# Two transformer layers on one core: fixed instruction orders, 76 instead of 50 score tiles on VectorE, elementwise work shared with GpSimd

## The chip, the cores and the metric

The kernel runs on one core of one Trainium2 chip. The metric is device microseconds from launch to end. TensorE (PE in the profile), ScalarE (ACT), VectorE (DVE), GpSimd (POOL) and SyncE (SP) each take their own list of instructions in order; semaphores connect the lists.

## The reference

`x` has 2048 rows of 448, in bf16. Attention has 16 heads of 28.

```python
x = A_x
x = x + _A_ref(_layernorm(x), A_wqkv, A_wo)              # attention
x = x + _B_ref(_layernorm(x), B_w1, B_w2, B_w3, B_w4)    # token mixer, MLP
...
scores = jnp.einsum("bhqd,bhkd->bhqk", q, k) * (Dh ** -0.5)
p = _softmax(scores, axis=-1)
o = jnp.einsum("bhqk,bhkd->bhqd", p, v)
...
h = _gelu(_layernorm(x) @ w1)       # then four column groups, shifted by -1, 1, -2, 2 rows
x1 = x + hs                         # hs = shifted h @ w2
h2 = _gelu(_layernorm(x1) @ w3) @ w4
return x1 + h2
```

The pair of lines on `x` is done twice, with the same weights: layers 0 and 1.

## The kernel before, in words

**Work.** The 2048 rows are 16 tiles of 128. Layer by layer, rows are normed, transposed and projected to qT, kT (heads in strips of 32 partitions, four heads to a group g) and vaug (v with a column of ones, which gives the softmax sum). Queries are taken in units u of 512 rows (the last 512 of the last layer in halves of 256). A segment is one unit, one group of four heads and a range of keys. For each 128 keys and each head PE makes a score tile of 128 keys by 512 queries (L1243); the tile is exponentiated into PT in bf16; PE multiplies it with vaug and gathers the result in bank 5 (L1318). When a segment ends, `t_norm` takes the sums out, transposes them, divides, and `t_outproj` multiplies by `wo` and adds to `x_res`. Then the mixer (`t_mixA`: norm, w1, gelu by `tanh_gelu`; `t_x1`: w2, norm) and the MLP (`t_mixB`: w3, gelu in place on ScalarE, w4) follow for that unit, while the attention of the next unit or the next layer runs.

**Exponentials.** Score tiles go in groups of alternately three and two into PSUM banks 0 to 2 and 3 to 4 (bank 5 takes the sums); one ScalarE instruction exponentiates a group (L1269), 128x1536 or 128x1024. In some groups of three the third tile is taken by VectorE instead (`t_dexp`, L1156): L1159 reads the bank and makes an integer of the score, L1166 cuts out its fraction, L1167 and L1168 evaluate a cubic, L1172 puts the bf16 bits together in PTD. ScalarE then has a 1024-column instruction for that group. `OFFL` and `on_dve` (L1132) choose these groups: every sixth or eighth in some ranges, 50 in all. Scores of group n+2 go into the banks of group n, the third only after L1159 has read its tile.

**Order.** All steps are generators that yield operations with the engine, an assumed duration, and what they read and write. `Sched.run` (L319) takes the operations greedily, in an order of due times that two rounds of planning give (`latest_starts`); `MOVES` and `perturb` (L455) shift due times by recorded random numbers. Buffers and PSUM banks are taken in the order in which the planner gets to them. `Plan.finalize` then sets the semaphores; there is no wait but for a true dependency, so SP and the others run ahead as far as their list and its waits allow. `keep_pe_busy` (L291) fills planned gaps of PE with products of ones (L1686, 128x256), at most to 0.8 of a window of 4 us.

**POOL before** makes the -1/2 powers of the norms (L1028, L1447, L1470, L1568), some masks and memsets. Norms of rows are L886 (`norm_x`), L1473, L1542 and L1572, residual adds L1392, L1570 and L1633, the division L1365, and the tanh polynomial L1419, L1420 and L1422 with L1437 after ScalarE's tanh (L1433), all on VectorE. `mm` (L665, L668) records the plain products, as one of 128 columns or, when PE is in column mode, as four of 32.

**Loads.** SP issues in order: x of the first four tiles, wk, wq, wv, the rest of x; later `wo` and the weights of mixer and MLP at given segments (`t_setup2`).

Of the kernel before, what the change touches and what calls it, by code (L numbers as in the profile page):

```python
# [17 lines left out]
class _Op:  # L18
    __slots__ = ("eng", "fn", "deps", "sig", "cnt", "waits", "dma", "ekey", "vc", "sem", "t_end", "pos", "every", "oid", "dur", "lft", "lst")

    def __init__(self, eng, fn, dma):
# [16 lines left out]
        self.lst = None  # L38


def _split(acc):
    if isinstance(acc, tuple) and len(acc) == 2 and isinstance(acc[0], tuple):
        return acc
    return acc, None


class Plan:
# [67 lines left out]
    def finalize(self, nc, stack):  # L115
# [4 lines left out]
        nd = 0  # L120
        for e in ENGS:
# [28 lines left out]
    def emit(self, eng_name, e):  # L150
        for op in self.ops[eng_name]:
# [5 lines left out]
            if isinstance(inst, list):  # L157
                first, inst = inst[0], inst[-1]
# [9 lines left out]
class Sched:  # L168
# [8 lines left out]
    def __init__(self, P):  # L177
# [4 lines left out]
        self.pe_mode = None  # L182
        self.act_tab = None
# [8 lines left out]
        self.fill = None  # L192
        self.recent = []
        self.clock = 0.0
        self.plan = None
        self.moves = []
# [3 lines left out]
    def spawn(self, gen, prio=5, order=None, parent=None):  # L200
        self.seq += 1
        if parent is None:
            tid = (self.seq,)
        else:
            parent[7] += 1
            tid = parent[6] + (parent[7],)
        self.tasks.append([prio, self.seq if order is None else order + self.seq * 1e-6, gen, None, None, False, tid, 0, 0, None])

    def rank(self, t):
        if self.plan is None:  # L210
            return (t[0], t[1])
        return (self.plan.get((t[6], t[8]), 1e9), t[1])
# [4 lines left out]
    def _advance(self, t, force=False):  # L217
        changed = False
        while True:
# [39 lines left out]
            elif c == "acq":  # L259
# [22 lines left out]
                t[4] = got  # L282
# [8 lines left out]
    def keep_pe_busy(self, until):  # L291
        if self.fill is None:
            return
        dur, fn, banks, key, reads = self.fill
        while self.cur["pe"] + dur + 0.12 < until:
# [21 lines left out]
            self.pe_mode = "plain"  # L317

    def run(self):  # L319
        P = self.P  # L320
        while True:
            while self.moves and self.clock >= self.moves[0][0]:
                self.perturb(self.moves.pop(0)[1])
# [23 lines left out]
            for t in self.tasks:  # L347
# [5 lines left out]
                for a in kw0.get("alt", ()):  # L353
                    cands.append(a)
# [8 lines left out]
                for ci, (eng, dur, fn, kw) in enumerate(cands):  # L363
# [13 lines left out]
                    if ci > 0 and (self.cur[eng] > ready + 0.05 or eng in self.reserved):  # L377
                        continue
# [57 lines left out]
            op = P.add(eng, fn, reads, writes, kw.get("deps", ()), dma, t_end)  # L436
            self.live.update(k for k in (_split(a)[0] for a in writes) if k[0] == "ps")
            self.live.difference_update(kw.get("last", ()))
            op.oid = (t[6], t[8])
# [15 lines left out]
    def perturb(self, seed):  # L455
        rng = random.Random(seed)
        if rng.random() < 0.2:
            self.SLACK = rng.choice((0.0, 0.06, 0.12, 0.3))
            self.TOL = rng.choice((0.0, 0.5, 1.5, 4.0))
            self.EPS = rng.choice((0.02, 0.05, 0.12))  # L460
        t = self.clock - self.shift
        lo, hi = t - 30.0, t + rng.choice((10.0, 25.0, 50.0, 90.0))
        depth = rng.choice((0, 1, 2, 3, 9, 9))
        width = rng.choice((1.0, 3.0, 8.0, 20.0))
        frac = rng.choice((0.05, 0.2, 0.5, 1.0))
        plan = self.plan
        sh = {}
        for k, v in plan.items():
            if lo < v < hi and k is not None:
                g = k[0][:depth] if depth else k  # L470
                d = sh.get(g)
                if d is None:
                    d = sh[g] = rng.gauss(0, width) if rng.random() < frac else 0.0
                if d:
                    plan[k] = v + d
# [21 lines left out]
def build_kernel(nc, A_x, A_wqkv, A_wo, B_x, B_w1, B_w2, B_w3, B_w4, out, n_layers=2):  # L497
    S = A_x.shape[1]
    D = 448
# [12 lines left out]
    OFFL = ((48, 104, 6), (104, 300, 6), (372, 411, 6), (480, 520, 6), (520, 600, 8), (640, 731, 6))  # L512
# [6 lines left out]
    MOVES = [  # L519
        [  # L520
# [50 lines left out]
    def c_f2b(n):  # L571
        return 0.07 + n * 0.00052
# [1204 lines left out]
```

## Time and profile before

| | us |
|---|---|
| median of three runs | 1059.28 |
| lowest and highest | 1057.09, 1060.65 |
| profiled execution, first to last instruction | 1059.8 |
| PE busy | 1020.3 |
| ScalarE busy | 1015.2 |
| VectorE busy | 744.5 |
| GpSimd busy | 57.8 |

The page gives for each engine its busy time; then the chain that ended last; then groups of instructions as "line engine operation, output <- inputs, shape, count | busy, mean ns | idle time of the engine just ahead of them, and who ended it". A table by stage gives each engine's busy time between two times. A PE product's end is modelled, so PE's share is less sure than the others'.

### The profile page before, as it was taken

How to read it: one execution, taken by the hardware profiler on the slowest of the kernel's cores; microseconds unless marked ns; L12 is line 12 of the kernel's file. 1: busy time of each engine (PE TensorE's matmuls, PEld its weight loads, DVE VectorE, ACT ScalarE, POOL GpSimd, SP SyncE). 2: the span in 40 equal slices, each digit the busy share in tenths (PEclk: the TensorE clock that was granted, in tenths of full speed). 3: DMA queues.
4: the chain of work that ended last, by engine and by line, in shares of the span. 5: the costliest groups of instructions: out<-in, count | busy, mean ns of one | idle time of the engine just before them, and what ended most of it. 6: DMA issues, size and time to landing. Idle time of an engine off the chain costs nothing.

```text
span 1059.8 us, 22773 instructions
## 1 busy us (share of the span) xinstructions
PE 1020.3 (96%) x9869; PEld 397.8 (38%) x9883; DVE 744.5 (70%) x1686; ACT 1015.2 (96%) x933; POOL 57.8 (5%) x80
## 2 busy tenths in 40 slices
PE   9999999999999999999999999989999999999998
PEld 5333332333333333333443443323333333434456
DVE  7966579866987547887689657785879645666454
ACT  5999999999999999999999999999999999999983
POOL 2000000100000001010101000000010000010000
PEclk8999999999999999999999999989999999999999
DMA  4243141001101002110111103211010100110000
GB/s 116 63 122 87 36 122 21 2 16 20 21 2 21 1 1 42 36 21 2 21 41 32 29 8 81 81 41 41 21 36 2 20 15 19 21 22 1 15 6 23
DMA packets 70717, 35.14 MB, mean 33 GB/s; under 512 B 56472, under 2 KB 65048, under 8 KB 70616
## 3 DMA queue, kind: packets, MB, share of 16 engines
q1 hardware_dynamic: 70616, 33.68, 13.4%
q8 instruction: 77, 1.26, 0.5%
q14 instruction: 24, 0.20, 0.1%
HBM read 12.70 MB, written 7.08 MB: 19 GB/s over the span
## 4 chain that ended last, share of the span: by engine, by line
ACT 52%; PE 41%; DVE 4%; DMA 1%; issue 1%; SPq 0%; POOLq 0%; POOL 0%; DVEq 0%
ACT PT L1269 45%; PE ps L1243 11%; PE ps L1318 9%; PE ps L665 9%; PE ps L1686 6%; ACT h2T L1650 4%; PE ps L916 3%; PE ps L668 3%; ACT gt L1433 1%; ACT L1650 1%; ACT L1269 1%; DVE kT L925 1%; DMA xT<-xn 1%; DMA wk_raw<-in_A_wqkv_dram 1%; DVE h2T L1609 0%
## 5 line engine op out<-in xcount | busy, mean ns | idle before, releaser
L1269 ACT ACTIVATE PT<-ps 128x1024 bf16<-128x1024 f32 (+1 forms) x821 | 917.2, 1225 | 10.2 <-PE ps L1243 6.4
L1243 PE MATMUL ps<-qT,kT 32*128 32x512 bf16 x1536 | 240.0, 386 | 13.8 <-ACT PT L1269 11.3
L1318 PE MATMUL ps<-PT,vaug 128*32 128x512 bf16 (+1 forms) x2253 | 250.0, 362 | 2.8 <-ACT PT L1269 1.4
L1686 PE MATMUL ps<-ones_bf 128*128 128x256 bf16 x928 | 143.6, 279 | 2.8 <-DVE hot L698 1.1
L1243 PEld LDWEIGHTS ps<-qT,kT 32*128 32x128 bf16 x1536 | 58.6, 91 | 196.1 <-ACT PT L1269 113.7
L665 PE MATMUL ps<-xT,w 112*128 112x512 bf16 (+5 forms) x623 | 129.2, 325 | 0.5 <-DVE h2T L1609 0.2
L1318 PEld LDWEIGHTS ps<-PT,vaug 128*32 128x32 bf16 x2253 | 65.7, 94 | 118.2 <-issue 66.0
L1609 DVE CAST h2T<-ps 128x512 bf16<-128x512 f32 (+2 forms) x126 | 73.5, 583 | 48.2 <-PE ps L665 40.3
L1686 PEld LDWEIGHTS ps<-ones_bf 128*128 128x128 bf16 x928 | 77.4, 99 | 71.3 <-issue 50.8
L1243 PE MATMUL ps<-kT 32*128 32x256 bf16 (+1 forms) x768 | 80.1, 310 | 2.5 <-ACT PT L1269 1.6
L665 PE MATMUL ps<-w,h2T 128*128 128x448 bf16 x327 | 75.1, 354 | 4.8 <-ACT h2T L1650 3.5
L665 PEld LDWEIGHTS ps<-xT,w 112*128 112x128 bf16 (+1 forms) x623 | 50.2, 103 | 53.6 <-issue 27.7
L1159 DVE TENSOR_SCALAR t<-ps 128x512 int32<-128x512 f32 x50 | 34.2, 684 | 34.4 <-PE ps L1243 34.0
L668 PE MATMUL ps<-xT,w 112*32 112x512 bf16 (+4 forms) x612 | 51.5, 337 | 0.0
L916 PE MATMUL ps<-xT,wq_raw 112*32 112x512 bf16 (+1 forms) x576 | 46.8, 367 | 1.9 <-DVE kT L925 0.9
L1243 PEld LDWEIGHTS ps<-kT 32*128 32x128 bf16 x768 | 21.4, 91 | 64.1 <-ACT PT L1269 32.8
L1650 ACT ACTIVATE h2T<-h2T 128x7168 bf16<-128x7168 bf16 (+2 forms) x9 | 44.8, 5010 | 0.1
L1340 DVE STREAM_TRANSPOSE u_sb<-ps 128x512 f32<-128x512 f32 (+1 forms) x24 | 15.0, 626 | 41.2 <-PE ps L1318 41.2
L916 PE MATMUL ps<-xT,wk_raw 112*32 112x512 bf16 (+3 forms) x640 | 41.8, 346 | 0.8 <-DVE vaug L983 0.3
L665 PEld LDWEIGHTS ps<-w,h2T 128*128 128x128 bf16 x327 | 27.9, 98 | 35.1 <-issue 11.7
L1568 POOL TENSOR_TENSOR mst<-mst,neghalf 128x1 f32<-128x1 f32 x32 | 24.3, 762 | 294.6 <-DVE mst L1566 266.5
L815 DVE BATCH_NORM_STATS2 st<-x_res 128x6 f32<-128x448 bf16 x64 | 38.7, 612 | 1.2 <-DMA x_res<-in_A_x_dram 0.6
(145 smaller groups left out, 1065.2 us busy)
## 6 DMA issues: line engine op xcount, KB each, us to landing
uin<-uscr SPq DMA_DIRECT2D x20, 256.0 KB, 2.6
uscr<-u_sb SPq DMA_DIRECT2D x12, 256.0 KB, 2.0
uscr<-uin SPq DMA_DIRECT2D x8, 256.0 KB, 2.0
out_dram<-uin SPq DMA_DIRECT2D x16, 112.0 KB, 1.7
w<-in_B_w_dram SPq DMA_DIRECT2D x4, 392.0 KB, 4.0
x_res<-in_A_x_dram SPq DMA_DIRECT2D x3, 448.0 KB, 8.9
w<-in_B_w_dram SPq DMA_DIRECT2D x2, 448.0 KB, 7.1
w<-in_B_w_dram SPq DMA_DIRECT2D x4, 196.0 KB, 2.8
```

The costliest lines, as they stand in the source:

```text
L665: return e.matmul(out=dst(0, m), lhsT=lhs(0, m), rhs=rhs, start=start, stop=stop)
L668: return [e.matmul(out=dst(a, min(m, a + 32)), lhsT=lhs(a, min(m, a + 32)), rhs=rhs, start=start, stop=stop, tile_position=(0, a)) for a i ...
L815: yield op("dve", 0.55, lambda e: e.bn_stats(out=st6[:, t, :], in_=x_res[:, t, :]), reads=[("x", t)], writes=[("st6", t)])
L916: yield op("pe", c_mm(nw) + Sched.COLT, lambda e, b=b, fc=fc, rows=rows: [e.matmul(out=ps[32 * j:32 * j + 32, bi(b), 0:nw], lhsT=w[0:rows, ...
L1159: yield op("dve", 0.06 + c_ps(512), lambda e: e.tensor_scalar(out=t32[:, :], in0=ps[:, bk, :], scalar1=0.0, scalar2=65536.0, op0=ALU.max, ...
L1243: yield op("pe", 0.005 if ph == h else 0.012 + W / 2400.0, lambda e, bk=bk, r0=32 * j, g=g, kc=kc, qt=qt, q0=q0, W=W, c0=W * h: e.matmul(o ...
L1269: yield op("act", e_dur(n), lambda e, b0=b0, p0=p0, cnt=cnt: e.activation(out=PT[:, p0:p0 + cnt, :], in_=ps[:, b0:b0 + cnt, :], func=ACT.E ...
L1318: yield op("pe", nt * 0.054 if item in late else 0.004 + nt * 0.0133, lambda e, j=j, rhs=rhs, vs=vs, i=i: e.matmul(out=ps[32 * j:32 * j + ...
L1568: yield op("pool", 0.57, lambda e, t=t: e.tensor_tensor(out=mst[:, t, R3:R3 + 1], in0=mst[:, t, V3E:V3E + 1], in1=neghalf[:, 0:1], op=ALU. ...
L1609: yield op("dve", c_ps(NW), lambda e, fch=fch, b=b: e.tensor_copy(out=h2T[:, fch, hoff:hoff + NW], in_=ps[:, bi(b), 0:NW]), reads=[("ps", ...
L1650: yield op("act", c_act(14 * NW), lambda e, c0=c0, NW=NW: e.activation(out=h2T[:, :, c0:c0 + NW], in_=h2T[:, :, c0:c0 + NW], func=ACT.Gelu ...
L1686: SC.fill = (0.13, lambda e, b: e.matmul(out=ps[:, bi(b), 0:256], lhsT=ones_bf[:, :], rhs=ones_bf[:, :].unsqueeze(1).to_broadcast([128, 2, ...
```

## The change

The order of every engine's instructions is now written out. `MOVES` and `perturb` go; after the two planning rounds `Sched.follow` (L582 of the changed file) takes each engine's list, reorders it by the numbers in `ENGINE_ORDER`, assigns buffers and banks anew as the lists get to them, and fills PE's gaps by a model of PE's four strips (`strip_time`). `OTHER` names 290 operations that leave the engine they were planned on for their alternative: GpSimd, or ScalarE for some copies. The tiles for VectorE stand in `DVE_TILES`, 76 of them, and no longer follow a stride. The slots of PTD, SQ, xn, xT and others are chosen by `follow`.

```diff
-    OFFL = ((48, 104, 6), (104, 300, 6), (372, 411, 6), (480, 520, 6), (520, 600, 8), (640, 731, 6))
+    DVE_TILES = frozenset((
+        54, 58, 66, 80, 84, 92, 96, 108, 114, 120, 132, 138, 144, 156, 162, 168, 174, 182, 186, 192, 198, 210, 216, 222, 234, 240, 246, 258, 264, 270, 276,
...
+        660, 668, 672, 678, 684, 696, 702, 708, 712, 720, 732, 760, 774, 788, 798))
...
-    MOVES = [
...
+    ENGINE_ORDER = {
+        "pe": (
+            "0 42 1 2 1 -2 1 -33 4 27 1 -36 3 5 2 19 1 -2 1 -26 1 7 3 17 1 -18 1 -16 1 -3 2 31 1 -35 1 13 1 4 5 1 7 4 1 -38 1 -2 1 -2 1 39 1 -14 1 17 1 -47 1 46 2 "
...
+    OTHER = (
...
             if isinstance(inst, list):
+                if eng_name != "pe":
+                    for a, b in zip(inst, inst[1:]):
+                        self.steps += 1
+                        a.then_inc(self.step_sem, 1)
+                        b.wait_op(self.step_sem, self.steps, "sem-ge")
                 first, inst = inst[0], inst[-1]
...
-        def on_dve(n):
+        def may_dve(n):
             if len(grans[n]) < 3:
                 return False
             L, u, g, p, kts, first, last = segs[grans[n][2][0]]
-            return 1 <= grans[n][2][1] <= len(kts) * UNITS[L][u][1] // 4 - 4 and any(a <= n < b and n % m == 0 for (a, b, m) in OFFL)
...
+            return 1 <= grans[n][2][1] <= len(kts) * UNITS[L][u][1] // 4 - 4
+
+        DVN = set(n for n in range(len(grans)) if may_dve(n) and n in DVE_TILES)
...
+            yield op("dve", c_f2b(512), lambda e: e.tensor_scalar(out=half(f), in0=lo, scalar1=EXPA * 2.0 ** -16, scalar2=None, op0=ALU.mult), reads=[("ti", ti)], writes=[("gt", f), ("gt", x)], pool=c_g1(512))
+            yield op("dve", c_ps(512), lambda e: e.scalar_tensor_tensor(out=half(x), in0=half(f), scalar=-EXPA, in1=half(f), op0=ALU.add, op1=ALU.mult), reads=[("gt", f)], writes=[("gt", x)], pool=c_g1(512) + c_g2(512), poolfn=lambda e: [
+                             e.tensor_scalar(out=half(x), in0=half(f), scalar1=-EXPA, scalar2=None, op0=ALU.add),
+                             e.tensor_tensor(out=half(x), in0=half(x), in1=half(f), op=ALU.mult)])
...
-                         reads=[("x", t), ("mv", t), ("rstd", t)], writes=[(xs.key, i)])
+                         reads=[("x", t), ("mv", t), ("rstd", t)], writes=[xs.part(i)], pool=c_g1(D))
...
-                     reads=[("x", t), ("x1b", s)], writes=[("x", t)])
+                     reads=[("x", t), ("x1b", s)], writes=[("x", t)], pool=c_g2(D))
...
-        for moves in MOVES[:-1]:
-            res = attempt(plan, moves)
-            plan = res[2].latest_starts(res[0])
-        est, P, SC = attempt(plan, MOVES[-1])
+        base = res[2]
+        est, P, SC = base.follow(ENGINE_ORDER, OTHER, MISC)
```

An operation with `pool=` may go to GpSimd; one that combines a scalar step and a product becomes two instructions there, the second waiting for the first (`step_sem`). In the built program 333 instructions are new on GpSimd: 55 pairs of polynomial steps of the VectorE tiles, 38 of their fractions, 42 row norms for the projections, 22, 21 and 15 of the mixer's norms, 19 residual adds, 23 divisions, and 43 of the tanh gelu. The arithmetic is otherwise as before.

529 lines of the change are left out of this document (374 added, 155 removed), and 275 rows, old and new, of tables (DVE_TILES, ENGINE_ORDER, MOVES, OTHER).

## The prediction, made before the run

> **What bounds the kernel now.** I read the page's busy shares first, then the busy time by stage, then ScalarE's groups by shape, then the two stretches in which ScalarE idles most.
>
> ```profile
> span 1059.8 us, 22773 instructions
> PE 1020.3 (96%) x9869; PEld 397.8 (38%) x9883; DVE 744.5 (70%) x1686; ACT 1015.2 (96%) x933; POOL 57.8 (5%) x80
> ACT 52%; PE 41%; DVE 4%; DMA 1%; issue 1%; SPq 0%; POOLq 0%; POOL 0%; DVEq 0%
> ```
> ```profile
> 0.00:27.20 27.20, 24.90 (x288) 14.32 (x289) 19.95 (x84) 14.46 (x20) 7.59 (x20) 0.87 0.43 113
> 27.20:1023.10 995.90, 963.45 (x9266) 361.79 (x9278) 706.01 (x1557) 984.57 (x875) 45.48 (x53) 1.00 0.13 32
> 1023.10:1059.80 36.70, 31.99 (x316) 21.65 (x316) 18.53 (x46) 16.14 (x40) 4.77 (x7) 0.99 0.05 17
> ```
> ```profile
> L1269 ACT ACTIVATE PT<-ps 128x1536 bf16<-128x1536 f32 x359 | 525.6, 1464 | 8.1 <-PE ps L1243 5.4 <-PE ps L1318 1.3
> L1269 ACT ACTIVATE PT<-ps 128x1024 bf16<-128x1024 f32 x459 | 467.0, 1042 | 2.0 <-PE ps L1243 1.0
> L1686 PE MATMUL ps<-ones_bf 128*128 128x256 bf16 x928 | 143.6, 279 | 2.8 <-DVE hot L698 1.1 <-DVE x_res L1392 0.5 <-DVE hT L1406 0.3
> L1243 PE MATMUL ps<-qT,kT 32*128 32x512 bf16 x1536 | 240.0, 386 | 13.8 <-ACT PT L1269 11.3
> ```
> PE and ACT both show 96%, but they are not equal. PE's 96% holds 143.6 us of filler (L1686, products of ones that nothing reads), so 877 us are work. ScalarE has no filler. The second table's columns are length, then busy time of PE, PEld, DVE, ACT, POOL, then granted clock. The stage of the exponentials runs from 27.2 to 1023.1 us, and there ScalarE works 984.57 of 995.90 us: 11.3 us idle. So **this stage lasts as long as ScalarE's list, plus what it waits**, and it waits for PE's scores (L1243). The start (27.2 us) waits for weights and the first projections, the end (36.7 us) for PE's last MLP products (31.99 us busy).
>
> ```profile
> 525.00:550.00 25.00, 24.46 (x317) 10.62 (x319) 21.00 (x57) 21.87 (x22) 1.33 (x2) 1.00 0.18 44
> 700.00:725.00 25.00, 23.14 (x222) 8.37 (x217) 18.93 (x42) 23.19 (x21) 0.00 (x0) 0.86 0.16 43
> ```
> Of those 11.3 us, 3.13 fall into the first of these stretches and 1.81 into the second, where the clock fell.
>
> **Part 1: 26 more tiles leave ScalarE.** In the built program ScalarE has 333 exponentials of 1536 columns instead of 359, and 485 of 1024 instead of 459. Each change saves 1464 − 1042 = 422 ns, so 26 × 0.422 = **11.0 us off the list that bounds the stage**. Nothing hides it while ScalarE stays the bound; what could be late next is PE's scores.
>
> ```profile
> L928 ACT ACTIVATE kT<-ps,cols 128x512 bf16<-128x512 f32 x3 | 2.3, 777 | 5.4 <-PE ps L916 5.3
> L987 ACT ACTIVATE vaug<-ps 128x448 bf16<-128x448 f32 x4 | 2.2, 544 | 0.9 <-PE ps L668 0.9
> ```
> One kT copy and one vaug copy now stand between exponentials instead of ahead of the first: 0.777 + 0.544 = **1.3 us back on**. ScalarE's other exchanges (three xT copies, two squares) lie ahead of the first exponential, where it idles 12.7 of 27.2 us: nothing.
>
> **Part 2: VectorE.** A tile costs it five instructions.
>
> ```profile
> L1159 DVE TENSOR_SCALAR t<-ps 128x512 int32<-128x512 f32 x50 | 34.2, 684 | 34.4 <-PE ps L1243 34.0
> L1166 DVE TENSOR_SCALAR gt<-t 128x512 f16<-128x512 uint16 x50 | 21.0, 420 | 1.0
> L1167 DVE SCALAR_TENSOR_TENSOR gt<-gt 128x512 f16<-128x512 f16 x50 | 34.4, 687 | 0.9
> L1168 DVE SCALAR_TENSOR_TENSOR gt<-gt 128x512 f16<-128x512 f16 x50 | 34.4, 687 | 1.0
> L1172 DVE SCALAR_TENSOR_TENSOR PTD<-t,gt 128x512 uint16<-128x512 int32 x50 | 34.4, 687 | 1.0
> ...
> L886 DVE TENSOR_SCALAR xn<-x_res,mv,rstd 128x448 bf16<-128x448 bf16 x56 | 20.2, 405 | 2.9 <-POOL rstd L1028 1.5 <-DMA xT<-xn 1.4
> L1542 DVE TENSOR_SCALAR x1b<-x_res,mv,mst 128x448 f32<-128x448 bf16 x32 | 15.5, 507 | 0.1
> L1570 DVE TENSOR_TENSOR x_res<-x_res,x1b 128x448 bf16<-128x448 bf16 x32 | 19.5, 610 | 0.0
> L1365 DVE TENSOR_TENSOR tn<-u_sb,rs 128x448 bf16<-128x448 f32 x28 | 17.4, 622 | 0.6
> L1420 DVE TENSOR_SCALAR gw<-gw 112x512 f16<-112x512 f16 x28 | 8.0, 286 | 0.4
> ```
> Added: 26 × (0.684 + 0.420 + 3 × 0.687) = 26 × 3.165 = 82.3 us. Given to POOL, counted in the built program: 55 of the 152 polynomial steps × 0.687 = 37.8; 38 of L1166 × 0.420 = 16.0; 42 of L886 × 0.405 = 17.0; 22 of L1542 × 0.507 and 21 like it (L1572) = 21.8; 19 of L1570 × 0.610 = 11.6; 16 of L1365 × 0.622 = 10.0; 15 norms of the mixer at L886's price = 6.1; the remaining 41 between L1420's 0.286 and L1167's 0.687, 12 to 28, I take 16. Together 136. VectorE goes from 744.5 to 744.5 + 82.3 − 136 = **691 us**, off the bound in either case: no term of the sum, but cover for Part 3's waits.
>
> **Part 3: GpSimd.** 333 more instructions, 64 of them a second half that waits for the first. No row of before shows such arithmetic on POOL.
>
> ```profile
> L713 POOL TENSOR_SCALAR_AFFINE_SELECT e<-ones_f 128x4 f32<-128x4 f32 x2 | 0.3, 191 | 0.0
> L709 POOL TENSOR_SCALAR_AFFINE_SELECT ident<-ones_bf 128x128 bf16<-128x128 bf16 x1 | 0.3, 298 | 0.6 <-DVE hot L698 0.6
> ```
> One input: (298 − 191)/124 = 0.86 ns an element, so 0.57 us at 448 and 0.63 at 512. Two inputs: between that and twice it (0.63 to 1.26 at 512); I take the upper end, two reads through one loop. About 217 one-input and 116 two-input instructions make 130 + (68 to 136): POOL goes from 58 to 256–324 us, at most 31%. Not the bound by itself. Behind its long instructions wait, in its queue, the pow steps of the norms (L1470, L1568), then VectorE or POOL for xn, and SP: most xT transposes now wait for POOL, with the uscr and uin transfers queued behind them.
>
> The two engines meet at SBUF:
>
> ```profile
> 201.30 0.86 POOL L1568 TENSOR_TENSOR mst<-mst,neghalf 128x1 f32<-128x1 f32 x1 [11.52 <-DVE mst L1566]
> 204.28 0.55 POOL L1568 TENSOR_TENSOR mst<-mst,neghalf 128x1 f32<-128x1 f32 x1 [2.12 <-DVE mst L1566]
> ```
> ```profile
> 201.14 0.62 DVE L1570 TENSOR_TENSOR x_res<-x_res,x1b 128x448 bf16<-128x448 bf16 x1
> ```
> ```profile
> L886 DVE TENSOR_SCALAR xn<-x_res,mv,rstd x4: 514/616/617, 24.7 to 26.2; 128x448 bf16<-128x448 bf16 x4
> ```
> ```profile
> L1473 DVE TENSOR_SCALAR xn<-x_res,mv,mst x32: 382/391/397, 168.8 to 1029.9; 128x448 bf16<-128x448 bf16 x32
> ```
> The same POOL instruction takes 0.86 us beside L1570 and 0.55 us without it; four VectorE norms beside POOL's memsets at 24.7 us took 616 ns where the same shape takes 391. So a meeting costs 0.23 to 0.31 us; 333 of them would put 333 × 0.225 = 75 us on VectorE, 766 us, still 73%. I cost this at nothing on the path; the price when that cover fails is rival D.
> The Trainium skill (SBUF — State Buffer, "Who interferes with whom") has it as an exclusive lock: a GpSimd instruction and a VectorE one with two SBUF inputs or in a two-port mode exclude each other for the whole instruction. The trace's 0.86 against 0.55 agrees; by that rule the time is rival D's.
>
> **Part 4: orders.** PE, ACT, DVE, POOL and SP follow fixed lists. PE changes between its modes (row strips, column strips, whole array) 1614 times instead of 1763, and the filler drops from 928 to 427 products. This can give back anything from all 11.3 us of idle to nothing, or lose more (C, D). The two stretches above (4.9 us) are single places whose order is written anew; I take 3.5 us back.
>
> SP now issues wv after 980 KB of weights of the MLP and after all of x:
>
> ```profile
> wv<-in_A_wqkv_dram SPq DMA_DIRECT2D x1, 392.0 KB, 7.7
> ```
> ```profile
> 2.86 0.49 SPq L787 DMA_DIRECT2D wv<-in_A_wqkv_dram  x1
> ```
> ```profile
> DMA packets 3522, 3.06 MB, mean 192 GB/s; under 512 B 128, under 2 KB 3520, under 8 KB 3520
> ```
> ```profile
> 12.86 3.56 PE ps L916 x25
> ```
> It landed at 2.86 + 7.7 = 10.6 us; now at most at (3.06 + 0.98) MB / 192 GB/s = 21 us. PE's list reaches it after 32 projections, at about 12.86 + 32/25 × 3.56 = 17.4 us. Between 0 and 3.6 us lost; I take **0.5**, since the first exponential comes only at 27.2. PE's work behind the last exponential is the same by count: 0 (±1.5).
>
> **Sum:** 1059.8 − 11.0 + 1.3 − 3.5 + 0.5 = 1047.1 us of span. The median of the three runs (1059.28) lies 0.5 under the profiled span, so **1046.5 us**.
>
> **The rivals.**
> B, *the lists leave no idle*: the whole 11.3 us go, 1059.8 − 11.0 + 1.3 − 11.3 − 0.5 = 1038.3. For it: ScalarE already runs stretches of dozens of exponentials without a gap. Against it: fixed lists meet durations that vary (0.55 or 0.86).
>
> C, *the clock falls more often*, for want of filler:
>
> ```profile
> 700.00:702.00 2.00, 1.21 (x12) 0.28 (x6) 1.93 (x4) 2.00 (x3) 0.00 (x0) 1.00 0.24 42
> 702.00:704.00 2.00, 1.22 (x13) 0.32 (x13) 1.97 (x6) 2.00 (x3) 0.00 (x0) 1.00 0.89 220
> 704.00:706.00 2.00, 2.00 (x8) 0.41 (x7) 2.00 (x6) 1.71 (x2) 0.00 (x0) 0.50 0.00 0
> ```
> PE was busy 2.43 of 4 us, then had half its clock, and that stretch cost ScalarE 1.81 us. Six such: 1046.5 + 6 × 1.8 = 1057.3. Against: 877 us of work in 1047 leave PE 84% busy without any filler.
> The Trainium skill (TensorE: Matmul & The Clock Gate, "Why this matters for your kernels") asks only that PE never idle for more than about 3 us. By it C would not happen, 1046.5 standing; this row shows a fall without such a gap, and the row decides.
>
> D, *the port makes VectorE's first step late, and the kernel slower.* The third score tile of group n+2 goes into the bank that L1159 reads for group n. L1159 may end 1.04 + 1.04 − 0.39 = 1.7 us after exponential n begins and takes 0.68: 1.0 us of slack. A VectorE instruction in front of it (0.69) that itself waits for a POOL pair member (up to 1.26) makes it 0.9 late, on average some 0.6, and ScalarE waits as long. The gain of 12.7 us is eaten from 21 of the 76 tiles on; at 32 the time is 1046.5 + 19.2 = 1065.7. For it: the rows at the port. Against it: in before VectorE waited 34.0 us for PE at L1159, not the other way.
>
> E, *ScalarE is not the bound after all* and PE's pace stays: 1059. That the tiles are not moved is excluded by the counts.
>
> **How the numbers follow.** Forecast 0.42 (own range 1040 to 1055), B 0.24, C 0.12, D 0.18, E 0.04. About 0.3% (3.2 us) is what a measurement of this kernel can tell from no change. Faster takes the forecast, B and part of C: 0.70. Within 0.3%: the rest of C and E: 0.11. Slower: D: 0.19. The range 1035 to 1066 leaves out the further half of D and little of B.
>
> **What would show it.** Right: ScalarE about 975 us busy in a stage that ends some 13 us earlier, idle under 11 us, 427 products of L1686's kind, clock 1.00 after 20 us. Wrong: ScalarE's idle above 24 us with L1159's successor released late (D), granted clock under 0.95 over the stage (C), wv as releaser of PE before 25 us (start), POOL near 400 us.

## The result and the profile of the changed kernel

The changed kernel takes **1211.1 us** (median of 4 runs, 1206.3 to 1219.3) against 1060.0 for the kernel before in the same job (4 runs, 1057.1 to 1063.0): a ratio of 1.143, 95% interval 1.140 to 1.147. The forecast of 1046.5 was wrong by 165 us, and the range with it.

Lines of the changed kernel: L1747 makes scores, L1773 exponentiates, L1806 multiplies by vaug; L1654 to L1673 are `t_dexp`, L1382 is `norm_x`, L1846 takes a segment's sums out of bank 5. The experiments' lines are shifted by some.

The page of the changed kernel: span, busy times, the row of the granted clock in 40 slices, and the shares of the chain that ended last.

```profile
span 1211.7 us, 23910 instructions
PE 1075.4 (89%) x10354; PEld 387.9 (32%) x10354; DVE 726.5 (60%) x1544; ACT 1017.5 (84%) x936; POOL 535.0 (44%) x413
PEclk8878799779986898999978899978679999978999
PE 34%; ACT 22%; POOL 21%; DVE 15%; DMA 4%; issue 2%; SPq 1%; POOLq 0%; DVEq 0%
```

POOL has 535 us where I had 256 to 324, and 21% of the chain; ScalarE fell from 52% of the chain to 22%. In the clock's row a 9 stands for 90% or more of full speed: 20 of the 40 slices lie below it, where the kernel before has two.

The three stages (start, exponentials, end) in the columns used for the kernel before:

```profile
0.00:25.80 25.80, 23.17 (x283) 14.32 (x287) 16.86 (x73) 14.64 (x20) 10.82 (x18) 0.87 0.56 158
25.80:1168.90 1143.10, 1018.10 (x9755) 350.89 (x9755) 694.42 (x1435) 988.42 (x877) 506.14 (x380) 0.89 0.11 27
1168.90:1211.70 42.80, 34.14 (x321) 22.65 (x320) 15.21 (x39) 14.48 (x39) 18.06 (x16) 0.96 0.06 17
```

The stage of the exponentials grew from 995.9 to 1143.1 us, with as much ScalarE work in it as before (988.4 against 984.6). So ScalarE stands 155 us in place of 11, at a mean clock of 0.89. (Counts times means of the exponentials fall from 1005.6 to 994.6 us, by the 11.0 of the forecast. The busy time doesn't follow: it counts overlapping instructions once, ScalarE's overlap by some 0.1 us where nothing is awaited between them, in all 97 us before and 85 here, and a wait takes that away.) For whom, the waits say (engine, line, releaser: us in total, times, longest):

```profile
ACT PT L1773 <- PE ps L1747: 117.3, 113, 9.8
ACT PT L1773 <- PE ps L1806: 18.6, 28, 2.2
...
DVE PTD L1673 <- POOL gt L1671: 48.4, 20, 7.2
DVE gt L1665 <- POOL gt L1664: 37.8, 25, 4.7
...
DVE gt L1668 <- POOL gt L1667: 18.3, 9, 4.4
DVE u_sb L1846 <- DMA uscr<-u_sb: 13.4, 2, 10.0
```

ScalarE waits for scores (117.3 us in place of 6.4), VectorE for POOL, at three places of the tile polynomial (104.5 us), and for a spill to memory (13.4 us, 10.0 of it in one piece). Why POOL is late stands in its groups (the column after the bar: busy us, mean ns of one):

```profile
L1382 POOL TENSOR_SCALAR xn<-x_res,mv,rstd 128x448 bf16<-128x448 bf16 x42 | 83.0, 1982 | 5.3 <-DMA xT<-xn 4.4
L1664 POOL TENSOR_SCALAR gt<-t 128x512 f16<-128x512 uint16 x38 | 57.3, 1508 | 151.4 <-DVE t L1654 144.9 <-DVE mst L1957 5.8 <-DVE hT L1947 0.6
L1670 POOL TENSOR_SCALAR gt<-gt 128x512 f16<-128x512 f16 x31 | 47.0, 1515 | 53.7 <-DVE gt L1665 39.9 <-DVE dcol L1575 12.6
...
L1671 POOL TENSOR_TENSOR gt<-gt 128x512 f16<-128x512 f16 x31 | 36.1, 1166 | 2.6
...
L1931 POOL TENSOR_SCALAR gw<-gw 112x512 f16<-112x512 f16 x14 | 12.2, 873 | 26.9 <-DVE gw L1930 26.6
```

One input at 448 takes 1.98 us (priced 0.57), at 512 1.51 (priced 0.63); two inputs 1.17, inside my bounds. But L1931, also one input, is much cheaper, and 0.62 us where VectorE does not disturb it (a row of POOL's timeline):

```profile
922.00 0.62 POOL L1931 TENSOR_SCALAR gw<-gw 112x512 f16<-112x512 f16 x1 [3.04 <-DVE gw L1930]
```

It does mult *and* add with constants; L1664 and L1670 do one operation, L1382 subtract and mult with two columns. That was my theory for the experiments: **the form of the instruction sets the price**.

How 1.9 us a norm in POOL's list become a wait of ScalarE can be followed at 744 us. Four timelines, of POOL, SyncE, PE and ScalarE (start, length, instruction, idle ahead of it and its releaser):

```profile
744.39 9.36 POOL L1382 TENSOR_SCALAR xn<-x_res,mv,rstd 128x448 bf16<-128x448 bf16 x5
```
```profile
753.78 1.95 SPq L1351 DMA_TRANSPOSE xT<-xn  x1
```
```profile
758.12 0.62 PE L1412 MATMUL ps<-xT,wk_raw 112*32 112x512 bf16 x4 [5.73 <-DMA xT<-xn]
```
```profile
760.82 1.45 ACT L1773 ACTIVATE PT<-ps 128x1536 bf16<-128x1536 f32 x1 [6.61 <-PE ps L1747]
```

Five norms on POOL end at 753.75; SyncE's transpose waits for the last and goes out at 753.78; PE, whose list has the projection ahead of the next scores, stands 5.73 us until it lands; ScalarE stands 6.61. At the 0.57 us that I had assumed, five norms would have ended 6.5 us sooner (9.36 − 5 × 0.57, an estimate), before PE came to them. From 756 to 762 us the granted clock is 0.50, so PE makes up nothing.

### The profile page after: what moved, and what is told of

Same layout as the page of the kernel before. It is cut to its first block, busy times and chain, and to the rows that moved or that the text cites. A ratio compares the mean times of both kernels' runs of the same rounds, so it can differ in the third digit from the quotient of the medians.

```text
span 1211.7 us, 23910 instructions
## 1 busy us (share of the span) xinstructions
PE 1075.4 (89%) x10354; PEld 387.9 (32%) x10354; DVE 726.5 (60%) x1544; ACT 1017.5 (84%) x936; POOL 535.0 (44%) x413
## 4 chain that ended last, share of the span: by engine, by line
PE 34%; ACT 22%; POOL 21%; DVE 15%; DMA 4%; issue 2%; SPq 1%; POOLq 0%; DVEq 0%
ACT PT L1773 20%; PE ps L1747 9%; PE ps L1149 8%; PE ps L1806 7%; PE ps L1152 5%; POOL xn L1382 4%; PE ps L1412 3%; POOL gt L1664 3%; DMA xT<-xn 2%; POOL x1b L2054 2%; POOL xn L2084 2%; DVE t L1654 2%; POOL gt L1670 2%; POOL xn L1985 2%; DVE PTD L1673 2%
## 5 line engine op out<-in xcount | busy, mean ns | idle before, releaser
L1773 ACT ACTIVATE PT<-ps 128x1024 bf16<-128x1024 f32 (+1 forms) x821 | 916.9, 1212 | 138.5 <-PE ps L1747 117.3
L1806 PE MATMUL ps<-PT,vaug 128*32 128x512 bf16 (+1 forms) x2222 | 306.8, 396 | 13.5 <-DVE u_sb L1846 6.6
L1747 PE MATMUL ps<-qT,kT 32*128 32x512 bf16 x1536 | 269.6, 421 | 42.4 <-ACT PT L1773 28.4
L1747 PEld LDWEIGHTS ps<-qT,kT 32*128 32x128 bf16 x1536 | 61.2, 92 | 267.9 <-ACT PT L1773 152.2
L1806 PEld LDWEIGHTS ps<-PT,vaug 128*32 128x32 bf16 x2222 | 84.4, 98 | 148.3 <-issue 101.2
L1664 POOL TENSOR_SCALAR gt<-t 128x512 f16<-128x512 uint16 x38 | 57.3, 1508 | 151.4 <-DVE t L1654 144.9
L1149 PE MATMUL ps<-xT,w 112*128 112x512 bf16 (+6 forms) x478 | 106.2, 336 | 5.2 <-DVE x1b L2073 1.6
L1152 PE MATMUL ps<-xT,w 112*32 112x512 bf16 (+3 forms) x1192 | 95.7, 366 | 7.5 <-DVE x1b L2073 3.3
L1747 PE MATMUL ps<-kT 32*128 32x256 bf16 (+1 forms) x768 | 87.0, 329 | 9.1 <-ACT PT L1773 5.8
L2196 PE MATMUL ps<-ones_bf 128*128 128x256 bf16 x427 | 87.6, 313 | 8.3 <-DVE x1b L2073 2.7
L1666 POOL TENSOR_SCALAR gt<-gt 128x512 f16<-128x512 f16 x24 | 36.2, 1506 | 123.5 <-DVE gt L1664 122.7
L1673 DVE SCALAR_TENSOR_TENSOR PTD<-t,gt 128x512 uint16<-128x512 int32 x76 | 57.4, 755 | 49.6 <-POOL gt L1671 48.4
L1382 POOL TENSOR_SCALAR xn<-x_res,mv,rstd 128x448 bf16<-128x448 bf16 x42 | 83.0, 1982 | 5.3 <-DMA xT<-xn 4.4
L1654 DVE TENSOR_SCALAR t<-ps 128x512 int32<-128x512 f32 x76 | 51.9, 684 | 37.5 <-PE ps L1747 36.7
L1670 POOL TENSOR_SCALAR gt<-gt 128x512 f16<-128x512 f16 x31 | 47.0, 1515 | 53.7 <-DVE gt L1665 39.9
L1152 PE MATMUL ps<-w,h2T 128*32 128x448 bf16 x972 | 59.4, 358 | 1.6 <-ACT h2T L2161 1.2
L2196 PEld LDWEIGHTS ps<-ones_bf 128*128 128x128 bf16 x427 | 37.2, 105 | 59.4 <-issue 27.2
```

The lines of the kernel that those rows point to most:

```text
L1149: return e.matmul(out=dst(0, m), lhsT=lhs(0, m), rhs=rhs() if callable(rhs) else rhs, start=start, stop=stop)
L1152: return [e.matmul(out=dst(a, min(m, a + 32)), lhsT=lhs(a, min(m, a + 32)), rhs=rhs() if callable(rhs) else rhs, start=start, stop=stop, t ...
L1382: yield op("dve", 0.21 + c_b2b(D), lambda e, t=t, i=i: e.tensor_scalar(out=blk(xs.v[:, i, :]), in0=b112(x_res[:, t, :]), scalar1=mv[:, t, ...
L1654: yield op("dve", 0.06 + c_ps(512), lambda e: e.tensor_scalar(out=t32[:, :], in0=ps[:, bk, :], scalar1=0.0, scalar2=65536.0, op0=ALU.max, ...
L1664: yield op("dve", c_f2b(512), lambda e: e.tensor_scalar(out=half(f), in0=lo, scalar1=EXPA * 2.0 ** -16, scalar2=None, op0=ALU.mult), reads ...
L1673: yield op("dve", 0.06 + c_ps(512), lambda e: e.scalar_tensor_tensor(out=PTD[:, to.n, :].bitcast(mybir.dt.uint16), in0=t32[:, :], scalar=2 ...
```

## The experiments

Fifteen runs. All but the first, which is another kernel, are compared with the kernel before on the same chip (its medians there: 1060.2 to 1061.7). "Plan" is the time that the kernel's own planner gives an operation.

**m1: the forms by themselves.** A kernel with loops over the forms; what it leaves out stands in the expectation.

> A kernel of its own that computes nothing of the reference (it copies x to the output): eight or more of each form of GpSimd's arithmetic, first with VectorE idle, then VectorE alone, then both together. Theory (the form of the instruction sets GpSimd's price): mult followed by add with two constants takes 0.6 to 0.7 us at 128x512, as the undisturbed rows of L1931 in the changed kernel do (0.62 us at 112x512); one operation alone takes 1.5 us, subtract and mult with two columns takes 1.85 us at 128x448, both with VectorE idle. Rival (VectorE's traffic slows GpSimd): with VectorE idle all forms take 0.57 to 0.75 us, and only the part with both engines busy shows 1.5 us. For the part with both engines: by the theory VectorE's three-operand instruction (0.69 us alone) takes 1.1 to 1.5 us beside the slow form; with the quick form I expect 0.7 to 1.2 us.

Measured, VectorE idle: POOL's groups by line. L271, 273 and 275 are one operation with a constant, L272, 274 and 276 the same data with two (mult and add, or add and mult); L280 and 283 are subtract and mult with two columns, L281 and 284 mult and add with two columns; L277 and 278 are L273 and 274 at half the width; L279 multiplies two tiles.

```profile
L271 POOL TENSOR_SCALAR g<-t 128x512 f16<-128x512 uint16 x8 | 11.8, 1508 | 2.1 <-DVE t L262 2.1
L272 POOL TENSOR_SCALAR g<-t 128x512 f16<-128x512 uint16 x8 | 4.7, 622 | 0.0
L273 POOL TENSOR_SCALAR g<-gi 128x512 f16<-128x512 f16 x8 | 11.7, 1492 | 0.1
L274 POOL TENSOR_SCALAR g<-gi 128x512 f16<-128x512 f16 x8 | 5.0, 621 | 0.6
...
L277 POOL TENSOR_SCALAR g<-gi 128x256 f16<-128x256 f16 x8 | 6.6, 865 | 0.0
L278 POOL TENSOR_SCALAR g<-gi 128x256 f16<-128x256 f16 x8 | 3.3, 407 | 0.6
L279 POOL TENSOR_TENSOR g<-gi,gj 128x512 f16<-128x512 f16 x8 | 8.9, 1153 | 0.1
L280 POOL TENSOR_SCALAR xn<-x,col 128x448 bf16<-128x448 bf16 x8 | 14.8, 1870 | 0.0
L281 POOL TENSOR_SCALAR xn<-x,col 128x448 bf16<-128x448 bf16 x8 | 5.6, 736 | 0.0
```

The rival falls: with VectorE idle the prices are those of the changed kernel. The form decides: 1492 ns for one operation, 621 for two with constants (add then mult as well: L276, 628); 1870 for subtract and mult with columns, 736 for mult and add: 2.4 and 2.5 times. Between 256 and 512 columns the single operation costs (1492 − 865)/256 = 2.45 ns an element and the pair (621 − 407)/256 = 0.84. No run has the columns with another pair of operations, so whether the subtraction itself is what is slow there stays open. One expectation missed: beside the slow form VectorE was not slowed at all (681 ns, expected 1.1 to 1.5 us); the last section has these rows.

**e1, e2, e3: all, or a part, taken back.** `follow` lays the kernel out once as changed, then gives the named operations back to VectorE, at the place in its list where they ran, and keeps every buffer:

```diff
-    def follow(self, order, other, banks):
+    def follow(self, order, other, banks, back=()):
...
+        made, home = self.lay(ops, after, seq, banks)[3:]
+        turn = {op: k for k, op in enumerate(made)}
+        for op, (eng, spec) in was.items():
+            if op.spec[1].__qualname__.split(".")[2] in back or spec[1].__qualname__.split(".")[2] in back:
+                op.eng, op.spec = eng, spec
+        for e in ("dve", "pool"):
+            seq[e] = sorted((op for op in ops if op.eng == e), key=lambda op: turn[op])
```

> The changed kernel with all 269 operations that it gave to GpSimd taken back to VectorE, put into VectorE's list where they ran by the plan; 76 tiles, the lists of TensorE, ScalarE and SyncE, and the buffers as in the changed kernel. Theory (GpSimd's operations run 2.4 to 3.3 times the time that the plan gives them, so that everything behind them comes late): most of the loss is gone, 1045 to 1075 us, with a granted clock above 0.97 and GpSimd below 100 us; VectorE then works 800 to 840 us. Rival one (too little filler, so the clock falls by itself): the clock stays below 0.93 and the time above 1130. Rival two (76 tiles are too many for VectorE, GpSimd or not): above 1100, with ScalarE or TensorE waiting for VectorE, which is then the engine that works most.

> The changed kernel with only the tile polynomials (38 fractions L1664, 55 pairs L1666 to L1671; 204 us of GpSimd's 535) taken back to VectorE; norms, residual adds and the tanh polynomials stay on GpSimd. Theory: these stand between a score tile and the product that reads it, so they carry the larger half of the loss: 1080 to 1140 us, GpSimd about 330 us, clock 0.93 to 0.97. If it is the norms and what queues behind them that carry the loss, 1150 to 1200. Rival (filler): above 1180 with a clock of 0.88 to 0.90.

> The changed kernel with only the 100 norms (L1382, L1985, L2054, L2084; 197 us of GpSimd's 535) and the residual adds L2082 taken back to VectorE; the tile polynomials and the tanh polynomials stay on GpSimd. Theory: 1110 to 1170 us, the smaller half of the loss, GpSimd about 320 us. If the norms carry the loss: 1060 to 1110. Rival (filler): above 1180.

| | us | clock | POOL, VectorE busy us |
|---|---|---|---|
| changed kernel | 1211.1 | 0.887 | 535, 727 |
| e2, polynomials back (one run) | 1165.0 | 0.915 | 327, 769 |
| e3, norms and adds back (one run) | 1128.6 | 0.945 | 321, 756 |
| e1, all back | 1101.7 | 0.95 | 55, 810 |

e1 is 1.036 of the kernel before (1.031 to 1.041). Taking GpSimd's work back brings 109 us of the loss of 151. It isn't the only thing that moves: the plan, with VectorE's prices, also puts more filler into PE's list (513 products in e1, 437 in e2, 466 in e3, against 427); by e5 and e11 below, which add 290, that is worth some 1 to 2 us. The two halves are not as I expected: the norms (with the residual adds) carry more, 82 us against 46, though 1128.6 lies in the range that I had set for the smaller half. e2 lies 25 us above its range. The two add up to more than the whole (128 against 109), so they overlap. PE's waits fit the path at 744 us:

```profile
PE ps L1412 <- DMA xT<-xn: 11.1, 4, 5.7
```
```profile
PE ps L1439 <- DMA xT<-xn: 10.8, 3, 5.8
```

The first row is of the changed kernel, the second of e2, where the norms are still on GpSimd; in e3 and e1 PE waits for no transpose. These waits are far less than 82 us. Half clock, as after the wait at 752 us, is a likely multiplier, but no run separates the two. And e1 isn't the 1045 to 1075 of the theory, nor its clock the 0.97: 41 us have another cause. At 1101.7 it even lies in the range of rival two (above 1100: too many tiles for VectorE), which e6 and e12 settle.

**e4: all on GpSimd, in the quick forms.** Constants as mult by 1 and add; norms as x·r + (−m·r).

```diff
-  e.tensor_scalar(out=half(x), in0=half(f), scalar1=-EXPA, scalar2=None, op0=ALU.add)
+  e.tensor_scalar(out=half(x), in0=half(f), scalar1=1.0, scalar2=-EXPA, op0=ALU.mult, op1=ALU.add)
...
+  e.tensor_scalar(out=nm[:, k:k + 1], in0=mean, scalar1=rs_, scalar2=-1.0, op0=ALU.mult, op1=ALU.mult)
+  e.tensor_scalar(out=out, in0=src, scalar1=rs_, scalar2=nm[:, k:k + 1], op0=ALU.mult, op1=ALU.add)
```

> The changed kernel, with the same 269 operations on GpSimd, but each in the form that run m1_pool_forms found quick: constants as mult by 1 and add; the norms as mult by r and add of -m*r, whose column a further GpSimd instruction of one element makes. Lists, tiles, buffers and filler are those of the changed kernel. By the measured prices GpSimd's work falls from 535 us to about 340 (tile polynomials 204 to 122, norms 197 to 90). Theory (GpSimd's late list is what the changed kernel pays): 1085 to 1135 us, clock above 0.93, ScalarE's wait for scores below 60 us. Rival (that VectorE and GpSimd meet at all is what costs, whatever the form; the quick form stretched VectorE's three-operand instruction from 0.68 to 1.07 us): above 1150. If GpSimd's price were all of the loss, this kernel would come to the 1047 that I forecast; the run e1_all_back (1101.7 without GpSimd) speaks against that.

1119.7 us (1109.1 to 1121.5), ratio 1.051 (1.045 to 1.058). Its page and POOL groups:

```profile
PE 1023.5 (92%) x10354; PEld 380.7 (34%) x10354; DVE 726.3 (65%) x1544; ACT 1009.6 (90%) x936; POOL 361.8 (32%) x513
```
```profile
L1389 POOL TENSOR_SCALAR xn<-x_res,rstd,nm 128x448 bf16<-128x448 bf16 x42 | 32.9, 783 | 4.2
L1676 POOL TENSOR_SCALAR gt<-t 128x512 f16<-128x512 uint16 x38 | 23.7, 622 | 173.6 <-DVE t L1666 166.9 <-DVE mst L1969 6.1 <-DVE hT L1959 0.6
```

The same 269 operations, the same lists, buffers and filler (427 products): the form alone is **91 us of the 151**. ScalarE's wait for scores falls from 117.3 to 55.8 us. All of this is as expected, and the rival (the meeting of the engines, whatever the form) falls as the main cause.

**e5, e6, e6b: where do e1's 41 us come from?** e5 fills PE's planned gaps more densely; e6 drops the written lists for the planner's own order, and e6b does that with the old 50 tiles.

```diff
-    TARGET = 0.8
+    TARGET = 1.1
...
-        while self.cur["pe"] + dur + 0.12 < until:
+        while self.cur["pe"] + dur < until:
```
```diff
-        est, P, SC = base.follow(ENGINE_ORDER, OTHER, MISC)
+        est, P, SC = attempt(plan, True)
```

> Run e1_all_back (all arithmetic on VectorE, 1101.7 us, clock 0.95) with more filler products in TensorE's list, 803 in place of 513: filler goes into every planned gap that holds one, without the margin of 0.12 us and the bound of 80%. What is asked is where e1's remaining 41 us come from. Theory (TensorE has too few products in the list to keep its clock where it waits): 1060 to 1085 us, clock 0.97 or more. Rival (the lists let TensorE stand at places where the plan saw no gap, and filler isn't put there): 1090 to 1115, clock 0.94 to 0.96.

> The changed kernel's 76 tiles with the order that the planner itself finds, as the kernel before had it (without its searched perturbations), in place of the written lists; all arithmetic on VectorE. Theory (what is left in e1_all_back is the written lists, made for a GpSimd that doesn't exist): 1050 to 1080 us. Rival (76 tiles are too many for VectorE): 1090 or more, and the next run clearly faster.

> The same with the 50 tiles of the kernel before. By the theory 1060 to 1085, up to 11 us above the run with 76 tiles (26 tiles of 0.42 us more on ScalarE). By the rival it is the faster of the two by 15 us or more.

One run each: e5 1097.9 us (clock 0.97), e6 1089.2, e6b 1103.5 (both 0.992). e5 has the clock of its theory and the time of its rival, 4 us below e1's median and inside the spread of e1's runs (1094.2 to 1105.3): more filler mends the clock and little of the time. That the clock is mostly a consequence of the waits is my reading; no run changes it alone. e6 is 12 us below e1 but 9 outside its range, and e6b is 18 above its own. Against e1 both change buffers, SyncE's order and filler too (1095 and 1209 products), so they do not price the lists by themselves. The pair settles one thing: with one planner, 76 tiles are 14.3 us faster than 50, though VectorE then works 804.5 us in place of 738.2. Too many tiles is not the cause. The pages of e6 and e6b:

```profile
PE 1041.8 (96%) x9924; PEld 411.9 (38%) x9924; DVE 804.5 (74%) x1826; ACT 1000.3 (92%) x923; POOL 58.6 (5%) x80
```
```profile
PE 1053.5 (96%) x10299; PEld 423.6 (38%) x10299; DVE 738.2 (67%) x1696; ACT 1011.3 (92%) x923; POOL 57.0 (5%) x80
```

ScalarE works 11.0 us less with 76 tiles, as Part 1 has it.

In e1's trace ScalarE's longest pause then pointed at SyncE. VectorE, ScalarE and SyncE around it:

```profile
70.40 0.69 DVE L1873 COPY u_sb<-ps 128x512 f32<-128x512 f32 x1 [6.30 <-DMA uscr<-u_sb]
```
```profile
72.34 2.37 ACT L1800 ACTIVATE PT<-ps 128x1024 bf16<-128x1024 f32 x2 [6.15 <-PE ps L1774]
```
```profile
62.05 1.49 SPq L1317 DMA_DIRECT2D w<-in_B_w_dram  x3
63.58 0.47 SPq L1317 DMA_DIRECT2D wo_pad<-in_A_wo_dram  x1
64.08 0.36 SPq L1887 DMA_DIRECT2D uscr<-u_sb  x1
```

Three weights and a part of wo (196 + 448 + 392 + 98 KB) go out just ahead of the spill of `u_sb`, which lands 6.3 us after its issue in place of the median 2.3; u_sb isn't free until then, so bank 5 isn't either, and ScalarE stands 6.15 us. Something like it happens to a load of `uin` at 100 us (4.2 us).

**e8 to e11: the spills first.** Two moves in SyncE's list, then with e5's filler, and with the quick forms on GpSimd:

```diff
+        sp = seq["sp"]
+        sp.insert(18, sp.pop(22))
+        sp.insert(30, sp.pop(35))
```

> Run e1_all_back (1101.7 us) with two moves in SyncE's list: the spill uscr<-u_sb that stood behind four weight loads (w1, w4, w3, wo_pad) is put ahead of them, and the load uin<-uscr that stood behind five of them (wo_pad, w3 twice, wo_pad, w4) ahead of those. In e1 VectorE waits for these transfers 6.3 and 4.2 us in one piece (u_sb and uin), and ScalarE stands 6.9 and 5.2 us at these places in the sister run with more filler. Theory (SyncE's new order puts the weights ahead of transfers that the attention waits for): both waits are gone, 1087 to 1094 us. Rival (the products are late there for another reason): the wait moves to another releaser, 1097 to 1103.

> The changed kernel (1211.1 us) with these two moves in SyncE's list and nothing else. VectorE there waits 13.4 us for uscr<-u_sb (10.0 in one piece) and 4.9 us for uin<-uscr. Theory: 1192 to 1203 us. Rival (hidden behind GpSimd's delays, which are larger there): 1205 to 1212.

> Run e8 (all arithmetic on VectorE, the two moves in SyncE's list) with the denser filler of run e5. Theory: 1080 to 1089 us, clock 0.975 or more. The kernel before (1060) it doesn't reach: what is left then is the order on TensorE and VectorE, with VectorE working 810 us in place of 744.

> Run e4_quick_forms (all 269 operations on GpSimd in the quick forms, 1119.7 us) with the two moves in SyncE's list and the denser filler of run e5. Theory (four causes that add: the form, the spills, the clock, and VectorE held by GpSimd at the port): spills 10 to 14, filler 4 to 8 less, 1097 to 1106 us. If GpSimd in the quick form were as good as hidden, it would beat e11_back_spills_filler; I expect it to stay 10 to 20 us above that one.

| | us (4 runs) | ratio to before, 95% | clock |
|---|---|---|---|
| e8, e1 with spills first | 1090.9 | 1.029 (1.025 to 1.032) | 0.958 |
| e9, changed kernel with spills first | 1201.5 | 1.134 (1.127 to 1.140) | 0.908 |
| e11, e8 with filler | 1083.5 | 1.022 (1.017 to 1.026) | 0.981 |
| e10, e4 with both | 1092.8 | 1.031 (1.028 to 1.034) | 0.966 |

The first three are as expected: SyncE's order costs 11 us in e1 and 10 in the changed kernel, filler 7. In e8 VectorE's wait for uin is gone and that for the spill is down to 2.6 us (7.7 in e1); in e9, where the loss of 10 us stands against runs that spread by 16, the spill still costs 8.2 (13.4 before). e10 came out 4 us better than expected, and stays 9 above e11 where I expected 10 to 20: GpSimd in the quick form is still no gain here. Whether by the port, by the longer way through two lists or by the filler (675 products in e10, 803 in e11), no run separates.

**e12: lists for VectorE's prices.** e11 has everything named so far mended and is 22 us above the kernel before. The written lists had been made for a GpSimd at a third of its time. e12 keeps e11's engines, tiles and buffers and takes new orders for PE, ScalarE, VectorE and GpSimd, from a search over single moves in the lists that counts all arithmetic at VectorE's price.

```diff
+            for e, text in (again or {}).items():
+                seq[e] = reorder([op for op in ops if op.eng == e], text)
```

`again` holds the new lists (`AGAIN`); `follow` is called with them as one argument more.

> Run e11 (all arithmetic on VectorE, spills first, denser filler, 1083.5 us) with TensorE's, VectorE's, ScalarE's and GpSimd's lists ordered anew by a search that counts every operation at VectorE's price, on the engine where it now runs; 76 tiles, buffers and SyncE's list as in e11. Theory (what is left of the loss in e11 is that the written lists were made for a GpSimd that takes a third of the real time): the many waits of ScalarE of 0.3 to 1 us for scores go, 1045 to 1062 us. Rival (VectorE's 810 us cannot be laid beside 985 us of ScalarE, 76 tiles are too many without GpSimd): 1072 to 1085 us.

1056.3 us (10 runs, 1050.6 to 1064.3), ratio 0.997 (0.994 to 1.000): no difference from the kernel before, and 27 us below e11, with less filler (383 products against 803). The rival falls: VectorE's 807 us lie beside ScalarE's work. What the new lists mend can be the wrong price or the move itself: they are searched for arithmetic that is on VectorE again. No run has lists searched for GpSimd at its measured prices with the work left there, so whether the change could pay in that way stays open. The stage of the exponentials, and the waits at the start, in a run of 1052.9 us:

```profile
32.20:1015.60 983.40, 954.63 (x10610) 354.46 (x10609) 771.43 (x1689) 973.53 (x877) 46.74 (x53) 1.00 0.14 31
```
```profile
ACT xn L1711 <- DVE vpe L1709: 8.0, 1, 8.0
```
```profile
DVE st L1607 <- DMA x_res<-in_A_x_dram: 7.5, 3, 5.6
```

The stage is 983.4 us, 12.5 under the kernel before, where my sum had −11.0 + 1.3 − 3.5 = −13.2. But the first exponential comes at 32.2 us in place of 27.2.

**e13, e14: the start, and lists searched longer.** e13 puts the late loads of x and wv ahead of w4 and w1 again: where SyncE's list began x, wk, x, wq, x, w4, x, w4, x, w1, wv, it begins x, wk, x, wq, x, x, x, wv, w4, w4, w1. e14 has that and lists from a longer run of the same search.

> Run e12 (1056.3 us) with the start of SyncE's list put back to the order of the kernel before: the three late loads of x and wv ahead of the 980 KB of w4 and w1 that the change put between them. In e12 VectorE waits 7.5 us for x (5.6 in one piece), ScalarE 8.0 us behind it, and the exponentials begin at 32.2 us in place of 27.2, while their stage is 983.4 us long in place of 996.0. Theory (what e12 still loses is the start alone): 1047 to 1053 us. Rival (the x loads are late for another reason, or another transfer is then late): 1054 to 1060.

> The same start with lists from a longer run of the same search. All arithmetic on VectorE, 76 tiles. Theory: 1043 to 1052 us, 0.8 to 1.6% below the kernel before: about what the 26 tiles are worth (11.0 us) and a little of the 11 us of idle. Rival (the lists fit the plan and not the chip, so more search gives nothing): the same as e13 within 2 us.

e13: 1058.7 us (11 runs, 1048.9 to 1062.2), ratio 0.998 (0.995 to 1.001). As a time that is no difference from e12: both spread by 13 us, with the clock (e12's runs with 0.993 or 0.994 took 1050.6 to 1052.4 us, those with 0.974 to 0.982 took 1058.2 to 1064.3). In the trace the stage begins at 30.7 in place of 32.2. So the order of the loads is 1.5 of the 5 us, and my theory that it was all falls. The changed kernel itself, with the loads in e12's order, begins its stage at 25.8 us; so most of the delay came with e12's lists.

e14: **1043.0 us** (4 runs, 1042.2 to 1043.7), ratio 0.985 (0.984 to 0.987), clock 0.995 in each. It beats both kernels. Its page and stages:

```profile
PE 1008.5 (97%) x11116; PEld 393.3 (38%) x11126; DVE 806.7 (77%) x1813; ACT 999.7 (96%) x936; POOL 56.1 (5%) x80
```
```profile
0.00:30.30 30.30, 25.27 (x271) 16.19 (x272) 17.20 (x78) 14.55 (x20) 7.97 (x20) 0.83 0.51 143
30.30:1006.30 976.00, 950.61 (x10519) 354.81 (x10529) 771.45 (x1692) 970.50 (x877) 43.90 (x53) 1.00 0.13 31
1006.30:1041.90 35.60, 32.61 (x328) 22.34 (x327) 18.09 (x45) 14.70 (x40) 4.23 (x7) 1.00 0.07 21
```

ScalarE stands 5.5 of 976 us, and the clock doesn't fall in the stage. The start is still 3 us later than before, and VectorE still waits 4.3 us in one piece for x there; why stays open.

From the changed kernel to e14, each step a difference of medians: GpSimd's work back on VectorE −109, spills first −11, filler −7, new lists −27, the longer search with the loads moved −13. Each price holds in this order only: e4 shows that most of the first step can also be had by the form.

## Why the prediction was wrong

**What bounds the kernel: right for the kernel before, and not for the changed one.** ScalarE's list fills 984.6 of 995.9 us of the stage before and 970.5 of 976.0 in e14. In the changed kernel its waits are 155 us, and the chain that ends last lies more on PE (34%) than on ScalarE (22%), with POOL at 21%.

**Part 1, 26 tiles: right.** ScalarE has 485 and 333 exponentials, counts times means of them fall by 11.0 us, and between e6 and e6b it works 11.0 us less; their times differ by 14.3. The saving was lost under the waits.

```profile
L1773 ACT ACTIVATE PT<-ps 128x1024 bf16<-128x1024 f32 x485 | 489.9, 1040 | 79.2 <-PE ps L1747 64.5 <-PE ps L1806 13.6
L1773 ACT ACTIVATE PT<-ps 128x1536 bf16<-128x1536 f32 x333 | 488.2, 1466 | 59.3 <-PE ps L1747 52.9 <-PE ps L1806 5.1
```

The idle column is the story: 138 us in place of 10.

**Part 2: nearly right, with two errors that partly cancel.** VectorE works 726.5 us for 691 forecast. My sums took the length of each instruction, but VectorE's instructions overlap when they follow each other: in m1 twelve of 677 ns take 7.2 us, 0.60 each. So e1, which has the 26 tiles and nothing on GpSimd, is 65.9 us above the kernel before and not 82.3 (some 3 us of the gap are copies and squares that went to ScalarE), and what left counts for less than 136. The stretching beside POOL can be read by shape: the instructions that stayed on VectorE are together 26 us longer in the changed kernel than the same shapes in e1. I had put it at 75.

**Part 3: the step that failed,** in two places. First the price: "One input: (298 − 191)/124 = 0.86 ns an element, so 0.57 us at 448 and 0.63 at 512." Those rows are of another operation. The slope is that of mult and add with constants (0.84 in m1), not that of a single operation (2.45), and the price is 2.4 to 3.5 times too low for most of the one-input work that the change issues. I carried 0.57 to 0.63 as if it were measured and gave it no upper end; the sum of 256 to 324 us was 535. Secondly "I cost this at nothing on the path": I named what queues behind POOL (the powers, xn, SP's transposes, uscr and uin) and then let VectorE's spare time cover it. Spare time covers load, not order: what waited was PE, for a transpose that stood behind POOL's list (the chain at 744 us), and VectorE itself, 104.5 us in the polynomial. e4 shows that even at prices nearer to mine (POOL 362 us) the work on GpSimd isn't free: 1119.7, 18 us above e1, which has all of it on VectorE and 86 filler products more.

The Trainium skill (GPSIMD Engine Reference, "4.1 Engine selection") calls GpSimd's one-input work roughly line-rate. m1 comes near it for mult and add (0.62 us for L1166's shape, where VectorE takes 0.42), and is far from it for one operation (1.51 us).

**Part 4: failed in its size.** I took 3.5 us back from the new orders. They were made for prices that don't hold: with all arithmetic on VectorE, spills and filler mended, they still cost 27 us against lists searched for that. Of SyncE's list I priced wv behind 980 KB (0 to 3.6 us; the start is 25.8 us, earlier than before) and overlooked the same pattern at 64 and 97 us in e1, with a spill that holds a PSUM bank behind one group of weights and the load of uin behind the other: 10 us.

**Rival C** had the mechanism and neither count nor cause: six falls for want of filler; the trace has 27 stretches at half clock, 274 us in all (the kernel before 3, 16.5 us). More filler gave 4 to 7 us; e14 keeps 0.995 with 413 filler products, fewer than the changed kernel's 427. **Rival D** had the sign and part of the way: VectorE did wait for POOL's half of a pair, and PE for VectorE's first step.

```profile
PE ps L1747 <- DVE t L1654: 10.0, 9, 3.6
```

The kernel before has no such wait. But 10.0 us of PE's time are not 165, and the cause was the form more than the port. Its break-even at 21 tiles was not tested: in e6 and e6b no pair is on POOL. **The signs to watch** were right: POOL near 400, clock under 0.95, idle above 24 all came, at 535, 0.89 and 155. (In the chances, 0.08 of C and 0.04 of E make 0.12 and D is 0.18, where the sums say 0.11 and 0.19; nothing hangs on it.)

## What to carry to other kernels

An operation that no row shows on an engine has no price: bound it above by a multiple, not by the nearest row's slope, and put that upper bound on the path of whatever waits for it in order. A written order goes with the prices and the engines that it was made for; when one of them changes, order again before judging the idea (27 us between e11 and e12, whose lists were made for other prices and other engines at once). And where a one-operand step must be on GpSimd, price it in the form of mult and add, which was 2.4 times as fast here.

## What the runs showed of the hardware

- GpSimd's TENSOR_SCALAR at 128x512 takes 1492 ns with one operation and 621 with two; at 128x448 with two columns 1870 (subtract, mult) and 736 (mult, add). A one-element column operation takes 0.33 to 0.35 us (e4).
- Beside an unbroken row of VectorE's three-operand instructions (L295, 24 in 14.5 us) the slow form did not slow VectorE (681 ns against 677 alone) but waited itself: one GpSimd instruction, the only one that met this row, lasted 15.6 us. The quick form shares instead: VectorE 1092 ns (L301), GpSimd 936, a pair every 1.015 us. Alone and back to back they take 0.60 and 0.62 us, 1.22 one after the other, so part of the pair runs together.

```profile
L293 POOL TENSOR_SCALAR g<-gi x26: 1483/1490/15562, 133.7 to 184.4; 128x512 f16<-128x512 f16 x26
```
```profile
L295 DVE SCALAR_TENSOR_TENSOR w<-t,gj x24: 679/681/682, 133.4 to 147.2; 128x512 uint16<-128x512 int32 x24
```
```profile
L301 DVE SCALAR_TENSOR_TENSOR w<-t,gj x24: 628/1092/1092, 186.2 to 209.1; 128x512 uint16<-128x512 int32 x24
```

The three numbers are shortest, median and longest. The Trainium skill (SBUF — State Buffer, "Who interferes with whom") has a lock for the whole instruction, taken by whoever comes first. The 15.6 us agree with a lock that the other engine doesn't get between back-to-back instructions; the 1.015 us of a pair don't agree with one that is held from end to end.
